# Linear attention and a SiLU MLP on one core: the second matmul moved into its own chunk, and heads regrouped

## The chip, the cores and the metric

The kernel runs on one core of one Trainium2 chip. The metric is the device time of one execution in microseconds; the time before is the median of three runs. One further execution was recorded by the hardware profiler, and the profile's times are counted from the start of its span.

A core has five engines with instruction streams of their own, each strictly in order: TensorE (PE in the profile, its weight loads PEld), VectorE (DVE), ScalarE (ACT), GpSimd (POOL) and SyncE (SP, which here only issues DMAs). Sixteen DMA engines move data between DRAM and the on-chip memory SBUF for all issuing engines. Matmuls write to PSUM, which has eight banks of 512 float32 columns.

## The reference

```python
def _attn_ref(q, k, v):            # each (8, 8, 576, 64): batch, head, position, 64
    q_s = softmax of q over the last axis
    k_s = softmax of k over the positions (axis 2)
    kv = np.einsum('bhsd,bhse->bhde', k_s, v)
    return np.einsum('bhsd,bhde->bhse', q_s, kv)

def reference(q, k, v, moe_w_in, moe_w_out):
    x = attention, heads side by side          # 4608 tokens x 512
    h = x @ moe_w_in                           # 512 x 2048
    g = h * (1 / (1 + exp(-h)))
    return g @ moe_w_out                       # 2048 x 512, float32
```

The softmaxes are written out in the original with a maximum subtracted and 1e-9 added to the sum.

## The kernel before

**Attention, batch by batch.** `load` brings q, k and v of a batch as tiles of 128 partitions: eight heads are four groups (`NG`) of two, a group's first head lies in partitions 0 to 63 and its second in 64 to 127, and each partition holds nine positions of 64 numbers (2304 bytes in DRAM). `exp` (ACT) makes `eq` and `ek` in bfloat16, `qsum` (DVE) the sums of `eq` and their reciprocals, `qnorm` multiplies them in (DVE or POOL), `vcast` casts v and leaves a column of ones beside it. `tr_dma` (L119) transposes `eq` to `qT` by one DMA from SP; batch 0 is transposed on TensorE instead (`tr`, `trcopy`). `kv` (L144) multiplies `ek` with v: 18 matmuls over 64 partitions for each half `cc` of the groups, into `kvps`, which has two PSUM banks of its own. `kvcopy` (L157) divides by the key sums (the column of ones) and puts the two heads of a chunk on the diagonal of a 128x128 block of `kvbd`, one block for each of the four chunks `c` of the 512 features. `xt` (L172) multiplies `qT` with these blocks and so gives `XT`, the tokens' attention output with features in partitions; it writes PSUM tile `o1` (one bank), and ACT copies it.

**MLP, chunk by chunk of tokens.** There are nine chunks: chunk 0 is batch 0 (576 tokens, in parts of 320 and 256), chunk 1 has 448 tokens, the others 512. `mm1(t, fb)` (L196) is one unit of the first matmul: four matmuls into a bank `hps`, tanh on ACT, and a multiply on DVE that writes `GT` (L216). There are 16 units `fb` for a chunk. The second matmul also has 16 units of four matmuls for a chunk: `mm2(t, tb, part, nparts)` (L228) takes the four 128-token tiles `tb` one after the other, each in four quarters of the contraction, so that two banks `ops` suffice; chunk 0 alone uses `mm2_wide` (L323), which does all four tiles for one `fc` at a time. `store` (L243) evicts a finished tile and writes it out by two DMAs of 64 partitions each.

**The order is written out by hand** (`manual_schedule`). A list `units` holds mm1 and mm2 units: mm1(0), mm2(0) and mm1(1) stand one after the other, mm2(1) follows and its second half alternates with mm1(2); from chunk 3 on mm1(t) alternates with mm2(t-1), and mm2(8) comes last, alone. `plan_attn` (L376) hangs the steps of a batch's attention on units before the start of the chunk that needs them; each engine's stream, SP's and POOL's too, follows this order. PSUM is divided into three banks `hps` (also used by `tr` and chunk 0's `xt`), two `ops`, one `aps` (for `o1`) and two `kvps`.

**The weights** come by DMAs from POOL, which cast to bfloat16: `W1` in 16 DMAs of 64 partitions (L279), since a chunk's 128 rows belong to heads that aren't neighbours in `w_in`, then `W2` in four DMAs (L284). A one-element copy on POOL (L273) makes them wait for the first half of batch 0's v; another (L399) makes batch 1's loads wait for the last piece of W1. Batch 2's q is loaded next on SP, ahead of batch 1's transpose. `heat` (L291) issues matmuls on a zero tile at the start.

## Time and profile before

| | |
|---|---|
| median of three runs | 305.15 us (304.4 to 307.14) |
| the profiled execution | 307.5 us |
| its span, first to last instruction | 305.7 us |
| TensorE busy | 281.9 us, 92% of the span |
| DVE / ACT / POOL busy | 148.9 / 162.5 / 52.3 us |
| DMA | 46.34 MB, mean 152 GB/s |
| granted TensorE clock, mean | 0.983 |

The profile's page cuts the span into 40 slices and gives each engine's busy share in tenths (9 means 90% or more); the DMA row is the mean share of the 16 DMA engines. The answer by stretches gives, for each stretch of time, its length and then the busy time of PE, PEld, DVE, ACT and POOL with the number of instructions in brackets, the granted clock (1.00 is full speed), the DMA share (contended packets can bring it above 1) and the GB/s. The chain of work that ended last is followed back from the last instruction, each step to what released it: start, length and what it was. A row of the timeline has start, length, engine, line, operation, output and inputs, how many instructions were merged, and in brackets the idle time before the first of them and what ended it. A row of the DMA queues has packets, MB and the packets' time as a share of 16 engines; q1 is the queue of SP, q0 that of POOL. The busy time of TensorE counts the modelled ends of pipelined matmuls.

### The profile page before, as it was taken

The page shows a single profiled execution, that of the slowest core. Times are in us where ns is not written, and L with a number is a line of the kernel's source. Part 1 is how long each engine was busy: PE and PEld are TensorE (multiplying, and loading weights), DVE is VectorE, ACT ScalarE, POOL GpSimd, SP SyncE. Part 2 cuts the span into 40 slices and gives each one's busy share as a digit, 9 for nine tenths or more (in the row PEclk, how much of TensorE's full clock was granted, in tenths as well). Part 3 has the DMA queues.
Part 4 walks back from the last instruction along what each step waited for, and adds up shares of the span by engine and source line. Part 5 has one row for each costly group of instructions (what it writes and reads, how often), then busy time and mean ns, then how long its engine had stood idle before and what let it go on. Part 6 is the DMA issues. An engine that isn't in the chain of part 4 may idle for free.

```text
span 305.7 us, 4237 instructions
## 1 busy us (share of the span) xinstructions
PE 281.9 (92%) x1597; PEld 135.2 (44%) x1597; DVE 148.9 (49%) x280; ACT 162.5 (53%) x266; POOL 52.3 (17%) x52
## 2 busy tenths in 40 slices
PE   5679995878999799989999999999999999999993
PEld 1546642434444344444444444444444444444441
DVE  4858884277355666543564366343533343343200
ACT  4647741577585686644765566543363445443320
POOL 0753000025080251700080017000000000000000
PEclk9579999999999999999999999999999999999999
DMA  7999999998959905961496142115111111112122
GB/s 268 259 141 159 282 312 289 348 392 246 346 198 243 362 2 104 341 202 35 82 326 240 34 93 55 35 36 112 36 34 34 34 36 34 34 40 56 44 69 69
DMA packets 39268, 46.34 MB, mean 152 GB/s; under 512 B 18256, under 2 KB 22352, under 8 KB 39248
## 3 DMA queue, kind: packets, MB, share of 16 engines
q1 hardware_dynamic: 34832, 41.88, 45.7%
q0 software_dynamic: 4416, 4.20, 9.3%
q8 instruction: 12, 0.20, 0.3%
q14 instruction: 8, 0.07, 0.1%
HBM read 36.70 MB, written 9.44 MB: 151 GB/s over the span
## 4 chain that ended last, share of the span: by engine, by line
PE 74%; DMA 15%; DVE 4%; ACT 2%; POOL 2%; issue 1%; SPq 1%; ACTq 0%; DVEq 0%; POOLq 0%
PE ops L233 35%; PE hps L200 34%; DMA vt<-in_v_dram 8%; DMA W_58<-in_moe_w_in_dram 4%; DMA qT<-eq 3%; PE kvps L149 2%; POOL W_58 L279 1%; DVE GT L216 1%; DVE zq L103 1%; PE ops L329 1%; ACT sg L208 1%; ACT eq L89 1%; SPq L80 0%; DVE kvbd_62 L163 0%; ACT XT L192 0%
## 5 line engine op out<-in xcount | busy, mean ns | idle before, releaser
L216 DVE SCALAR_TENSOR_TENSOR GT<-sg,hps 128x512 bf16<-128x512 f32 (+2 forms) x176 | 100.4, 586 | 114.4 <-ACT sg L208 113.5
L200 PE MATMUL hps<-XT,W_58 128*128 128x512 bf16 (+3 forms) x640 | 147.0, 361 | 3.7 <-DVE GT L216 2.7
L208 ACT ACTIVATE sg<-hps 128x512 f32<-128x512 f32 (+3 forms) x160 | 88.3, 554 | 96.4 <-PE hps L200 94.9
L233 PE MATMUL ops<-W_59,GT 128*128 128x512 bf16 x512 | 128.6, 379 | 0.0
L200 PEld LDWEIGHTS <-W_58 128*128 128x128 bf16 x640 | 61.7, 99 | 70.0 <-issue 7.4
L233 PEld LDWEIGHTS <-GT 128*128 128x128 bf16 x512 | 48.9, 98 | 55.7
L109 POOL TENSOR_TENSOR eq<-eq,rzq 128x1152 bf16<-128x1152 bf16 x12 | 25.4, 2117 | 123.0 <-ACT eq L89 56.8
L248 ACT ACTIVATE ost<-ops 128x512 f32<-128x512 f32 x34 | 20.2, 598 | 19.4 <-PE ops L233 19.4
L103 DVE TENSOR_REDUCE zq<-eq 128x18 f32<-128x1152 bf16 x16 | 21.6, 1348 | 7.9 <-ACT eq L89 7.9
L89 ACT ACTIVATE ek<-kt 128x1152 bf16<-128x1152 f32 x16 | 18.4, 1156 | 5.7 <-DMA kt<-in_k_dram 5.7
L89 ACT ACTIVATE eq<-qt 128x1152 bf16<-128x1152 f32 x16 | 18.4, 1159 | 2.4 <-DMA qt<-in_q_dram 2.4
L149 PEld LDWEIGHTS <-ek 64*128 64x128 bf16 x288 | 9.2, 99 | 13.0 <-issue 6.9
L329 PE MATMUL ops<-W_59,GT 128*128 128x512 bf16 x64 | 14.9, 379 | 0.0
L279 POOL DMA_DIRECT2D W_58<-in_moe_w_in_dram x16 | 9.7, 642 | 3.2 <-DMA W_58<-in_moe_w_in_dram 3.1
L329 PEld LDWEIGHTS <-GT 128*128 128x128 bf16 x64 | 6.2, 98 | 8.9 <-issue 2.0
L149 PE MATMUL kvps<-vaug_61,ek 64*128 64x130 bf16 x144 | 5.5, 217 | 3.9 <-DVE vaug_61 L96 2.3
L149 PE MATMUL kvps<-vaug_60,ek 64*128 64x130 bf16 x144 | 6.4, 240 | 2.7 <-ACT vaug_60 L94 1.3
L96 POOL CAST vaug_61<-vt 128x1152 bf16<-128x1152 f32 x6 | 6.8, 1157 | 0.0
L96 POOL CAST vaug_60<-vt 128x1152 bf16<-128x1152 f32 x6 | 6.8, 1155 | 0.0
L293 PE MATMUL wps<-warm 128*128 128x512 bf16 x11 | 4.8, 599 | 1.2 <-DVE warm L258 1.2
L109 DVE TENSOR_TENSOR eq<-eq,rzq 128x1152 bf16<-128x1152 bf16 x4 | 5.4, 1357 | 0.1
L132 PE MATMUL qtps<-ident,eq 128*128 128x128 bf16 x18 | 2.3, 313 | 3.3 <-DVE eq L109 3.3
(137 smaller groups left out, 80.2 us busy)
## 6 DMA issues: line engine op xcount, KB each, us to landing
out_dram<-ost SPq DMA_DIRECT2D x72, 128.0 KB, 2.4
qt<-in_q_dram SPq DMA_DIRECT2D x7, 1152.0 KB, 6.5
kt<-in_k_dram SPq DMA_DIRECT2D x7, 1152.0 KB, 8.4
vt<-in_v_dram SPq DMA_DIRECT2D x7, 1152.0 KB, 11.7
W_58<-in_moe_w_in_dram POOLq DMA_DIRECT2D x16, 128.0 KB, 6.5
W_59<-in_moe_w_out_dram POOLq DMA_DIRECT2D x4, 512.0 KB, 14.5
qt<-in_q_dram SPq DMA_DIRECT2D x2, 576.0 KB, 4.1
kt<-in_k_dram SPq DMA_DIRECT2D x2, 576.0 KB, 7.4
```

The source lines that it names most:

```text
L89: nc.scalar.activation(out=o, in_=jgd(st[b][src], cc), func=ACT.Exp)
L96: eng.tensor_copy(o, jgd(st[b]["vt"], cc))
L103: nc.vector.reduce_sum(out=st[b]["zq"][:, cc], in_=e, axis=AX.X)
L109: eng.tensor_tensor(out=e, in0=e, in1=r[:, :, :, None].to_broadcast([128, J, 2, D]), op=ALU.mult)
L149: nc.tensor.matmul(out=st[b]["kvps"][:, r, cc * 256:cc * 256 + 2 * E1], lhsT=st[b]["ek"][r * P:(r + 1) * P, j, cc * 128:(cc + 1) * 128], r ...
L200: nc.tensor.matmul(out=hps[:, 0:size], lhsT=W1[:, c, fb * 128:(fb + 1) * 128], rhs=XT[t][:, c, off:off + size], start=(c == 0), stop=(c == ...
L208: nc.scalar.activation(out=sg[:, 0:size], in_=hps[:, 0:size], func=ACT.Tanh, scale=0.5)
L216: nc.vector.scalar_tensor_tensor(out=GT[g][:, fb, col:col + n], in0=sg[:, h], scalar=1.0, in1=hps[:, h], op0=ALU.add, op1=ALU.mult,)
L233: nc.tensor.matmul(out=OP[t, tb], lhsT=GT[t][:, fc, tb * 128:(tb + 1) * 128], rhs=W2[:, fc, :], start=(fc == 0), stop=(fc == NFB - 1),)
L248: nc.scalar.activation(out=ost, in_=OP[t, tb], func=ACT.Copy, scale=0.5)
L279: nc.gpsimd.dma_start(out=W1[g * 64:(g + 1) * 64, 2 * cc:2 * cc + 2, i * FQ:(i + 1) * FQ], in_=w_in_v[g][:, cc, :, i * FQ:(i + 1) * FQ],)
L329: nc.tensor.matmul(out=OP[t, tb], lhsT=GT[t][:, fc, tb * 128:(tb + 1) * 128], rhs=W2[:, fc, :], start=(fc == 0), stop=(fc == NFB - 1),)
```

## The change

- A unit of mm2 of chunk t now runs inside chunk t: mm1(t) leads by six units (`LAG`), then mm2 and mm1 units alternate. Chunk 0 does this by itself; chunks 1 to 8 run through in one alternating sequence.
- `mm2(t, i)` takes quarter `i // 4` of the contraction for tile `i % 4`, so that all four tiles are open at once in four banks `ops`, and all four finish in the last four units. Odd tiles are evicted by DVE, even ones by ACT. `mm2_wide` is gone.
- PSUM: four banks `ops` and one ring of four banks for everything else: `hps`, `o1`, `tr`'s tiles, and kv's result, which is now two tiles of one bank.
- `kvcopy` handles the two tiles separately: two reciprocals and four multiplies in place of one and two.
- Heads: chunk c now holds heads 2c and 2c+1, so a chunk's rows of `w_in` are 128 neighbouring rows. In return a load of q, k or v is cut into four DMAs of 64 partitions (two halves `cc`, two heads `r`). Batch 0's q and its first half of k are shared between the queues of SP and ACT.
- Weights: W1 in four DMAs of 128 partitions, in the order W1(0), W1(1), W2(0), W1(2), W2(1), W1(3), W2(2), W2(3). Batch 1's loads wait for W2(1).
- More `heat` matmuls (24, 5, 1 and 2 in place of 10 and 1), and other offsets for the attention steps; batch 1's `qnorm` goes to POOL, its `vcast` stays on DVE.

```diff
@@ -63,21 +63,17 @@
 
     ctx.enter_context(tc.manual_schedule())
 
-    def view(t, b, cc=None):
...
     st = [dict() for _ in range(B)]
 
-    def load(b, name, src, cc=None):
+    def load(b, name, src, ccs=(0, 1), engs=(nc.sync, nc.sync)):
         if name not in st[b]:
             st[b][name] = ld.tile([128, NG, J * D], FP32, name=name)
-        t = st[b][name]
-        if cc is None:
-            nc.sync.dma_start(out=t, in_=view(src, b))
-        else:
-            nc.sync.dma_start(out=t[:, 2 * cc:2 * cc + 2, :], in_=view(src, b, cc))
+        x = src[b].rearrange("(c r g) (p j) d -> c r p g (j d)", r=2, g=2, j=J)
+        for cc in ccs:
+            for r in range(2):
+                engs[r].dma_start(
+                    out=st[b][name][r * P:(r + 1) * P, 2 * cc:2 * cc + 2, :], in_=x[cc, r]
+                )
 
     def jgd(t, cc):
         return t[:, 2 * cc:2 * cc + 2, :].rearrange("p g (j d) -> p j g d", d=D)
@@ -125,7 +121,7 @@
     TG = 6
 
     def tr(b, g):
-        t = ps.tile([128, TG, 128], BF16, name="qtps", tag="hps", bufs=PSB["hps"])
+        t = ps.tile([128, TG, 128], BF16, name="qtps", tag="ring", bufs=PSB["ring"])
         st[b]["qtps", g] = t
         for i in range(TG):
             cc, j = divmod(g * TG + i, J)
@@ -142,12 +138,12 @@
             i += n
 
     def kv(b, cc):
-        if "kvps" not in st[b]:
-            st[b]["kvps"] = ps.tile([128, 2, 512], FP32, name="kvps", tag="kvps", bufs=1)
+        t = [ps.tile([128, 512], FP32, name="kvps", tag="ring", bufs=PSB["ring"]) for _ in range(2)]
+        st[b]["kvps", cc] = t
         for j in range(J):
             for r in range(2):
                 nc.tensor.matmul(
-                    out=st[b]["kvps"][:, r, cc * 256:cc * 256 + 2 * E1],
+                    out=t[r][:, 0:2 * E1],
                     lhsT=st[b]["ek"][r * P:(r + 1) * P, j, cc * 128:(cc + 1) * 128],
                     rhs=vaug[b % 2][r * P:(r + 1) * P, j, cc * 2 * E1:(cc + 1) * 2 * E1],
                     start=(j == 0),
@@ -155,26 +151,26 @@
                 )
 
     def kvcopy(b, cc):
-        kp = st[b]["kvps"][:, :, cc * 256:cc * 256 + 2 * E1]
-        rz = ap.tile([128, 2, 2], FP32, name="rz")
-        nc.vector.reciprocal(out=rz, in_=kp[:, :, D::E1])
-        for g in range(2):
-            h = slice(g * 64, (g + 1) * 64)
-            nc.vector.tensor_tensor(
-                out=kvbd[b % 3][h, 2 * cc:2 * cc + 2, g * 64:(g + 1) * 64],
-                in0=kp[h, :, g * E1:g * E1 + D],
-                in1=rz[h, :, g:g + 1].to_broadcast([64, 2, D]),
-                op=ALU.mult,
-            )
+        for r in range(2):
+            kp = st[b]["kvps", cc][r]
+            rz = ap.tile([128, 2], FP32, name="rz", bufs=4)
+            nc.vector.reciprocal(out=rz, in_=kp[:, D:2 * E1:E1])
+            for g in range(2):
+                h = slice(g * 64, (g + 1) * 64)
+                nc.vector.tensor_scalar_mul(
+                    out=kvbd[b % 3][h, 2 * cc + r, g * 64:(g + 1) * 64],
+                    in0=kp[h, g * E1:g * E1 + D],
+                    scalar1=rz[h, g:g + 1],
+                )
 
     XT = {}
 
-    def xt(t, c, tag="aps", dve=0):
+    def xt(t, c, tags=("ring", "ring"), dve=0):
         if t not in XT:
             XT[t] = mp.tile([128, NC, S], BF16, name="XT")
         cc, r = divmod(c, 2)
         for i, (off, size) in enumerate(part[t]):
-            o1 = ps.tile([128, TCH], FP32, name="o1", tag=tag, bufs=PSB[tag])
+            o1 = ps.tile([128, TCH], FP32, name="o1", tag=tags[i], bufs=PSB[tags[i]])
             a = first = cut[t] + off
             while a < first + size:
                 b, col = divmod(a, S)
@@ -195,7 +191,7 @@
 
     def mm1(t, fb):
         for off, size in part[t]:
-            hps = ps.tile([128, TCH], FP32, name="hps", tag="hps", bufs=PSB["hps"])
+            hps = ps.tile([128, TCH], FP32, name="hps", tag="ring", bufs=PSB["ring"])
             for c in range(NC):
                 nc.tensor.matmul(
                     out=hps[:, 0:size],
@@ -225,11 +221,13 @@
 
     OP = {}
 
-    def mm2(t, tb, part, nparts):
-        if part == 0:
+    def mm2(t, i):
+
+        qd, tb = divmod(i, 4)
+        if qd == 0:
             OP[t, tb] = ps.tile([128, DM], FP32, name="ops", tag="ops", bufs=PSB["ops"])
-        n = NFB // nparts
-        for fc in range(part * n, (part + 1) * n):
+        n = NFB // 4
+        for fc in range(qd * n, (qd + 1) * n):
             nc.tensor.matmul(
                 out=OP[t, tb],
                 lhsT=GT[t][:, fc, tb * 128:(tb + 1) * 128],
@@ -237,8 +235,8 @@
                 start=(fc == 0),
                 stop=(fc == NFB - 1),
             )
-        if part == nparts - 1:
-            store(t, tb)
+        if qd == 3:
+            store(t, tb, tb % 2)
 
     def store(t, tb, dve=0):
         ost = mp.tile([128, DM], FP32, name="ost", bufs=4)
@@ -251,18 +249,20 @@
             rows = out[b * S:(b + 1) * S, :].rearrange("(p j) o -> j p o", j=J)[col // P]
             nc.sync.dma_start(out=rows, in_=ost[i * P:(i + 1) * P, :])
 
-    PSB = {"hps": 3, "ops": 2, "aps": 1}
+    PSB = {"ring": 4, "ops": 4}
 
 
     nc.vector.memset(dummy, 0.0)
     nc.vector.memset(warm, 0.0)
     nc.scalar.activation(out=dummy, in_=dummy, func=ACT.Exp)
     make_identity(nc, ident_f)
+    both = (nc.sync, nc.scalar)
     for cc in range(2):
-        load(0, "qt", q, cc)
-    for cc in range(2):
-        load(0, "kt", k, cc)
-        load(0, "vt", v, cc)
+        load(0, "qt", q, (cc,), both)
+    load(0, "kt", k, (0,), both)
+    load(0, "vt", v, (0,))
+    load(0, "kt", k, (1,))
+    load(0, "vt", v, (1,))
     nc.vector.tensor_copy(ident, ident_f)
     for t in vaug:
         nc.vector.memset(t.rearrange("p j (g e) -> p (j g) e", e=E1)[:, :, D:E1], 1.0)
@@ -270,29 +270,41 @@
         nc.vector.memset(t, 0.0)
 
 
-    nc.gpsimd.tensor_copy(gate[:, 0:1], st[0]["vt"][0:1, 1, 0:1])
     FQ = DFF // 4
-    w_in_v = w_in.rearrange("(c g r d) f -> g d c r f", g=2, r=2, d=D)
-    for i in range(4):
-        for g in range(2):
-            for cc in range(2):
-                nc.gpsimd.dma_start(
-                    out=W1[g * 64:(g + 1) * 64, 2 * cc:2 * cc + 2, i * FQ:(i + 1) * FQ],
-                    in_=w_in_v[g][:, cc, :, i * FQ:(i + 1) * FQ],
-                )
-    for i in range(4):
+
+    def load_w1(i):
+        nc.gpsimd.dma_start(
+            out=W1[:, :, i * FQ:(i + 1) * FQ],
+            in_=w_in[:, i * FQ:(i + 1) * FQ].rearrange("(c p) f -> p c f", p=128),
+        )
+
+    def load_w2(i):
         nc.gpsimd.dma_start(
             out=W2[:, i * 4:(i + 1) * 4, :],
             in_=w_out[i * FQ:(i + 1) * FQ, :].rearrange("(fc p) o -> p fc o", p=128),
         )
 
+    nc.gpsimd.tensor_copy(gate[:, 0:1], st[0]["vt"][0:1, 1, 0:1])
+    load_w1(0)
+    load_w1(1)
+    load_w2(0)
+    load_w1(2)
+    load_w2(1)
+    load_w1(3)
+    load_w2(2)
+    load_w2(3)
+    st[1]["qt"] = ld.tile([128, NG, J * D], FP32, name="qt")
+    nc.gpsimd.tensor_copy(st[1]["qt"][0:1, 0, 0:1], W2[0:1, 4, 0:1])
+    for name, src in (("qt", q), ("kt", k), ("vt", v)):
+        load(1, name, src)
+
     wps = ps.tile([128, 512], FP32, name="wps", tag="ops", bufs=PSB["ops"])
 
     def heat(n):
         for _ in range(n):
             nc.tensor.matmul(out=wps, lhsT=warm[:, 0:128], rhs=warm, start=True, stop=True)
 
-    heat(10)
+    heat(24)
     for cc in range(2):
         exp(0, "qt", "eq", cc)
         qsum(0, cc)
@@ -303,77 +315,41 @@
     vcast(0, 1, nc.scalar)
     tr(0, 0)
     trcopy(0, 0)
+    heat(5)
     kv(0, 0)
     kvcopy(0, 0)
     heat(1)
     for g in (1, 2):
         tr(0, g)
         trcopy(0, g)
+    heat(2)
     kv(0, 1)
     kvcopy(0, 1)
     for c in range(NC):
-        xt(0, c, "hps", 1)
-
-
+        xt(0, c, ("ring", "ops"), 1)
+
+
+
+    LAG = 6
     units = []
 
-    def add_mm1(t):
...
-    add_mm2(NCH - 1)
+    def add(first, last):
+        x = [(("mm1", t), lambda t=t, i=i: mm1(t, i)) for t in range(first, last) for i in range(NFB)]
+        y = [(("mm2", t), lambda t=t, i=i: mm2(t, i)) for t in range(first, last) for i in range(NFB)]
+        units.extend(x[:LAG])
+        for i in range(len(y)):
+            units.append(y[i])
+            units.extend(x[LAG + i:LAG + i + 1])
+
+    add(0, 1)
+    add(1, NCH)
     begin = {t: next(u for u, f in enumerate(units) if f[0] == ("mm1", t)) for t in range(NCH)}
     at = [[] for _ in units]
 
     def plan(u, f):
         at[u].append(f)
 
-    def plan_attn(b, u, sm, tp, ks, ox, eng=(nc.gpsimd, nc.gpsimd)):
+    def plan_attn(b, u, sm, tp, ks, ox, eng=(nc.gpsimd, nc.gpsimd), veng=nc.gpsimd):
 
 
 
@@ -382,7 +358,7 @@
             plan(u + sm[cc] + 1, lambda cc=cc: (qsum(b, cc), qnorm(b, cc, eng[cc])))
         for cc in range(2):
             plan(u + sm[2 + cc], lambda cc=cc: exp(b, "kt", "ek", cc))
-            plan(u + sm[2 + cc], lambda cc=cc: vcast(b, cc, eng[cc]))
+            plan(u + sm[2 + cc], lambda cc=cc: vcast(b, cc, veng))
         plan(u + tp, lambda: tr_dma(b, nc.sync))
         if b == 1:
             plan(u + tp, lambda: [load(2, n, x) for n, x in (("kt", k), ("vt", v))])
@@ -394,19 +370,12 @@
         for c in range(NC):
             plan(u + ox[c], lambda c=c: xt(b, c))
 
-
-    st[1]["qt"] = ld.tile([128, NG, J * D], FP32, name="qt")
-    nc.gpsimd.tensor_copy(st[1]["qt"][64:65, 0, 0:1], W1[64:65, 3, DFF - 1:DFF])
-    for name, src in (("qt", q), ("kt", k), ("vt", v)):
-        load(1, name, src)
-    plan(14, lambda: load(2, "qt", q))
     V = nc.vector
-    plan_attn(1, begin[1], (-14, -12, -10, -9), -6, (-5, -4), (-4, -3, -2, -1), (V, V))
-    plan_attn(2, begin[2], (-21, -17, -13, -9), -9, (-7, -5), (-4, -3, -2, -1))
-    plan_attn(3, begin[3], (-26, -24, -22, -20), -13, (-9, -7), (-6, -5, -4, -3))
-    plan_attn(4, begin[4], (-42, -38, -34, -30), -20, (-12, -10), (-9, -7, -5, -3))
-    for b in range(5, B):
-        plan_attn(b, begin[b], (-56, -52, -48, -44), -22, (-13, -11), (-9, -7, -5, -3))
+    plan(begin[1] - 8, lambda: load(2, "qt", q))
+    plan_attn(1, begin[1], (-16, -14, -10, -9), -7, (-4, -3), (-3, -2, -1, 0), (nc.gpsimd, nc.gpsimd), V)
+    plan_attn(2, begin[2], (-27, -24, -20, -16), -14, (-9, -7), (-5, -4, -3, -2))
+    for b in range(3, B):
+        plan_attn(b, begin[b], (-48, -44, -40, -36), -22, (-15, -11), (-9, -7, -5, -3))
     for c in range(NC):
         plan(begin[NCH - 1] - 9 + 2 * c, lambda c=c: xt(NCH - 1, c))
 
```

## The prediction

> **What bounds the kernel now.** I read the page's 40 slices first (a slice is 7.64 us), then the stretches by stage, then the chain of work that ended last, then the DMA queues.
>
> ```profile
> PE   5679995878999799989999999999999999999993
> DMA  7999999998959905961496142115111111112122
> ```
> ```profile
> 38.20:58.50 20.30, 16.14 (x106) 7.56 (x104) 10.05 (x18) 7.04 (x11) 0.00 (x0) 1.00 1.10 305
> 58.50:73.80 15.30, 12.62 (x65) 6.18 (x64) 12.14 (x20) 11.72 (x20) 5.37 (x4) 1.00 0.95 353
> 73.80:84.30 10.50, 10.23 (x82) 5.00 (x81) 4.17 (x11) 6.00 (x11) 1.05 (x1) 1.00 1.03 311
> 84.30:110.30 26.00, 23.58 (x142) 10.98 (x141) 15.82 (x28) 18.39 (x29) 11.41 (x7) 1.00 0.73 233
> 110.30:135.00 24.70, 23.43 (x141) 11.00 (x140) 13.29 (x24) 15.29 (x24) 7.89 (x6) 1.00 0.61 190
> 188.00:218.00 30.00, 30.00 (x175) 14.04 (x174) 12.34 (x22) 14.95 (x26) 1.61 (x2) 1.00 0.26 55
> ```
>
> In the second fence the first figure after the stretch is its length, the next is TensorE's busy time. From 135 us to the last matmul TensorE is always busy: a chunk takes 30.0 us, and 32 units of 0.864 us (four matmuls of 512 columns, from the chain), two kv blocks of 0.69 and four xt of 0.22 make 29.9. Reordering can gain nothing there. All that can be won lies before 135 us: between 58.5 and 135 TensorE is idle for 2.68 + 0.27 + 2.42 + 1.27 = 6.6 us, and before 58.5 the DMA row is full. The chain says what the early part waits for:
>
> ```profile
> 22.14 5.55 DMA W_58<-in_moe_w_in_dram
> 29.12 16.71 DMA vt<-in_v_dram
> 45.84 8.44 DMA qT<-eq
> ```
>
> Chunk 1 needs batch 1, whose loads wait until all of W1 has landed (27.8 us), share the DMA engines with W2, and end at about 50.5; then the DMA transpose of qT lands at 54.3, and four xt, each followed by four matmuls, lead to chunk 1's first mm1 at 58.5. Whatever TensorE does faster before that only waits longer.
>
> **Part 1: the early order and the loads.** Chunk 0's second matmul now runs inside its first one. TensorE's work up to batch 1's xt is the same: from about 19.5 us (the first steady mm1 now is at 19.1), six units alone at 1.0 us, ten pairs at 0.97 + 0.86, three units, one kv: it stands still at about 47 to 49 us. So the start of chunk 1 (call it T1) stays a DMA sum, which I take from these rows.
>
> ```profile
> q0 software_dynamic: 2468, 2.27, 102.9%
> ...
> q0 software_dynamic: 372, 0.37, 113.4%
> ...
> q1 hardware_dynamic: 1091, 2.44, 58.9%
> q0 software_dynamic: 1091, 1.08, 53.1%
> ...
> q1 hardware_dynamic: 362, 0.80, 101.9%
> ```
>
> They are packets per queue in 12 to 28 us (W1 in 16 pieces), 30 to 32 (W2 in whole pieces), 32 to 44 (both queues) and 46 to 48 (loads alone). Without the packets under 512 B, weights go at 138 a us in 64-partition pieces, at 183 in whole ones; in the mix each queue moves 88 a us; loads alone 172. The weights are 4096 packets of 2 KB read, a batch's q, k and v 3 x 512 of 2304 B. W1 becomes whole, but keeps its strided rows, so I take 160 a us between the ends. Batch 1 is now released by the fifth of eight pieces, 2560 packets: 12 + 2522/160 = 27.8, landed 1.2 later as W1 is now, first load packet another 3.5 later (now: issue 28.0, packets from 31.5): 32.5. By then 3312 weight packets are through. The other 784 take 784/88 = 8.9 us, with as many load packets; then 1536 + 512 (batch 2's q stands ahead of the transpose on SP, as now) - 784 = 1264 at 172 take 7.3: 48.7, against 50.5 now, -1.8 us. At 138 the same sum gives 51.8 (+1.3), at 183 it gives 46.2 (-4.3). I take **T1 -1.5**, the mean of the ends, with both kept.
>
> Whether halves load as fast as whole tiles is the open price. A load of one tensor is now four DMAs of 64 partitions, not one of 128. The nearest rows are the output stores, which are 64 partitions already:
>
> ```profile
> DMA packets 464, 0.78 MB, mean 392 GB/s; under 512 B 91, under 2 KB 91, under 8 KB 463
> ...
> q1 hardware_dynamic: 463, 0.77, 101.7%
> ```
> ```profile
> DMA packets 160, 0.26 MB, mean 175 GB/s; under 512 B 32, under 2 KB 32, under 8 KB 160
> ...
> q1 hardware_dynamic: 160, 0.26, 75.1%
> ```
>
> The first is 69.5 to 71.5 us, stores in a backlog: 16 engines x 2 us x 1.017, less 91 small packets of 9 ns, over 372 packets is 85 ns for 2 KB. The second is 216.5 to 218, one pair of stores alone: 141 ns. Loads stand in a backlog, so I take the first row: no price. The other end, a factor 1.66 on a load packet's 93 ns, is a rival below. The Trainium skill speaks against the change here: "DMA: Bandwidth & Descriptors", section "Rules for kernel authors", says two transfers to disjoint partition halves serialize and one 128-partition transfer should be used, and "SBUF — State Buffer", section "Door 1: The DMA port swizzle", puts 64 partitions at 196 GB/s against 328. By that page the 1264 packets alone would cost some 62 ns each (93 x 328/196 - 93), an estimate of 4.9 us; the isolated pair agrees with it, the backlog row doesn't.
>
> The small edits of the start (14 + 5 + 2 more warm-up matmuls at 0.43 us cold or 0.22 warm, three loads issued on ACT, which is idle until 4.4 us, four-piece copies of kv) move TensorE's start by -0.5 to +4 us. The wait for qT, which I expect at 48.7 + 3.8 = 52.5, hides 3.5 us of that; beyond, it costs one for one. POOL issues 8 weight DMAs at 0.76 us in place of 16 at 0.64 and 4 at 0.76 (6.1 us for 13.3), ahead of nothing that is late. SP issues 12 DMAs a batch at 0.47 to 0.52 us (6 us, 288 KB each 0.5 us, more than the engines move), with the transpose and the stores behind them; the stores have four buffers and a chunk of time.
>
> **Part 2: from T1 to 135 us.** The idle 6.6 us come from stretches of mm1 without mm2:
>
> ```profile
> 66.68 3.19 PE L200 MATMUL hps<-XT,W_58 128*128 128x448 bf16 x16 [1.12 <-DVE GT L216]
> 70.93 3.19 PE L200 MATMUL hps<-XT,W_58 128*128 128x448 bf16 x16 [1.06 <-DVE GT L216]
> ```
>
> Here mm1 takes 0.756 us a unit, DVE 0.62, and a reduction with its reciprocal (1.35 + 0.27) stands between, so three hps banks run out. With the change only six such units stand alone after T1; then each has an mm2 unit beside it, and there are four banks. What is late next: in those six units DVE has 6 x 0.62 + 2 x 1.62 = 7.0 us of work against 4.5 of TensorE; four banks and the first mm2 leave about 1.5 us of stall. The crowded heads of batches 2 and 3 (two exp of 1.16 in one unit, xt in four consecutive units) leave another 1.1. So 2.6 of 6.6 stay: **-4.0**; bounds -1.5 (the crowd stays late) to -5.6 (1 us left).
>
> **Part 3: steady state.** Units, matmuls and pairing are as now. The ring of four holds hps, xt's o1 and two kv banks. kvcopy grows from 0.18 + 2 x 0.29 to 2 x 0.18 + 4 x about 0.21 (the 128x64 multiply at 37.86 us took 0.21): 1.2 us. Its wait stands on DVE ahead of the next GT multiply. Worst order: GT 0.69, reduction 1.62, kvcopy 1.2 = 3.5 us, against four units of 0.864 = 3.5 until the next kv wants the banks. So about 0, with 0.2 a kv at most; the 12 kv after T1 are inside Part 2's bounds.
>
> **Part 4: the end.** Now the four tiles of the last chunk finish 3.46 us apart; then 0.864 apart, with eight DMA issues of 0.515 us on SP, 4.1 us against 3.5, and the last eviction on DVE (0.69 for 0.60): **+0.7**, from 0 to +1.2.
>
> **Sum.** -1.5 - 4.0 + 0.7 = -4.8. The profiled execution took 307.5 us with a span of 305.7: 302.7. The median of the runs is 305.15, 2.35 below that execution; on its scale **300.4**. Bounds of this case: -9.9 to +1.0, 295 to 306.
>
> **Rivals.**
> - *Halves load at the slow rate.* For: the isolated pair of stores. Against: the backlog row. 1264 packets x 61 ns / 16 = +4.8 on T1, and batch 2's k, v and batch 3's loads come 2560 x 61 / 16 = 9.8 us late at exps that stand at most 8 us behind T1: some 2.5 us of ACT and then TensorE. 300.4 + 7.3 = 307.7. It cancels the gain from about 133 ns a packet.
> - *The ring stalls* (the slower side). kv takes two of four banks and returns them through DVE; if one reduction or one exp more comes ahead of kvcopy, the next kv or hps waits 1.2 to 1.6 us. At half of 12 kv, 6 x 1.4 = 8.4: 308.8. It decides from 0.4 us a kv, where 12 x 0.4 eat the 4.8. For: the same wait exists now at 100.7 us (1.53 us on kvbd). Against: Part 3's count.
> - *It doesn't do what it says.* The first chunks' idle time is that of batches 1 to 3 arriving late, and it moves instead of going: T1 0, -1.0, +0.7: 304.9. For: DMA is full until 75 us. Against: the waits above name DVE, not a load.
>
> **How the numbers follow.** Forecast 0.47, slow halves 0.20, moved idle 0.21, ring 0.12. About 1% (3.05 us) is what a measurement of this kernel can tell from no change. Faster: 0.43 of the forecast's case and 0.03 of the moved one, 0.46. Slower: 0.10 of the slow halves (with weights at 138 they give 310), 0.09 of the ring, 0.02 elsewhere, 0.21. The rest is 0.33. The range leaves out one in ten a side: 296 to 308.8.
>
> **What would show it.** First mm1 of chunk 1 near 57 us; load packets alone near 93 ns; hps waiting on GT under 3 us between T1 and 135 us; a chunk at 30.0 us; the last matmul some 5.5 us before the end. Wrong if load packets take over 130 ns, if kvps or o1 waits on DVE or ACT in every chunk, or if warm-up or batch 0 brings TensorE to batch 1's xt after qT has landed.

## The result, and the profile after

The changed kernel takes 314.75 us (median of 4 runs, 312.93 to 317.49); the kernel before took 305.52 us beside it (4 runs, 304.40 to 307.14). The ratio is 1.0305, with a 95% interval of 1.0215 to 1.0396. The forecast was 300.4 us, its range 296 to 308.8, so the measured time lies outside it. The rival *slow halves* named the right cause, with 307.7 us, and was still 7 us short. Of the ten executions of one kernel below (*before, four whole DMAs*) two ran in a slower state; its ratio leaves them out, its median doesn't.

In what follows a load in *halves* is one by DMAs of 64 partitions, as in the change, and a *whole* load one by DMAs of 128. T1 is the start of chunk 1's first mm1.

The profiled execution of the changed kernel was its fastest, 312.93 us, with a span of 311.2 us; that of the kernel before was 307.5 us with 305.7. These two traces differ by 5.5 us of span, less than the medians, and the first part of what follows explains 5.5 us. The experiments add the rest.

The page's slices come first (one is 7.78 us; DMA busy share in tenths):

```profile
PE   8559985889689999999999999999999999999992
...
DMA  7999999999999898289838974500450050014005
```

TensorE's row now has its weak slices at 2 and 3 (5 and 5; before, the weak ones were 1 and 2), the old hole at slice 7, and a new one at slice 11. The DMA row, which had its first gaps at slices 10 to 13 (8, 9, 5, 9), is now full to slice 13 and not under 8 until slice 17: the same 46 MB take longer. The chain of work that ended last says for whom (start, length, what):

```profile
30.63 6.29 DMA qt<-in_q_dram
...
36.94 11.34 DMA vt<-in_v_dram
...
48.34 9.47 DMA qT<-eq
...
61.91 8.74 DMA qt<-in_q_dram
...
70.67 8.58 DMA vt<-in_v_dram
...
79.27 1.93 DMA out_dram<-ost
...
81.67 4.77 DMA qT<-eq
```

Before, the chain ended its DMA part with batch 1's qT at 54.3 us. Now it goes through batch 1's qT at 57.8, and then through loads once more, to batch 2's qT at 86.4. TensorE's rows show both, and the row of before for T1 stands first (start, busy time, line, operation, in brackets the wait ahead of it and what ended it):

```profile
58.53 5.61 PE L200 MATMUL hps<-XT,W_58 128*128 128x448 bf16 x28
```
```profile
53.06 1.55 PE L145 MATMUL kvps<-vaug_61,ek 64*128 64x130 bf16 x18 [3.01 <-DVE GT L212]
...
57.94 0.35 PE L178 MATMUL o_724<-qT,kvbd_63 128*128 128x448 bf16 x1 [0.88 <-DMA qT<-eq]
...
61.88 4.16 PE L196 MATMUL hps<-XT,W_58 128*128 128x448 bf16 x20
...
86.48 0.32 PE L178 MATMUL o_1020<-qT,kvbd_64 128*128 128x384 bf16 x1 [3.81 <-DMA qT<-eq]
```

T1, the first mm1 of chunk 1, is at 61.88 us (58.53 before): +3.35. From T1 to the last matmul's end it is 243.5 us against 242.3: +1.2. From there to the end 5.8 against 4.85: +1.0. Together 5.5.

**Loads run at three fifths of their speed.** The DMA view of 40 to 50 us, where batch 1's loads are nearly alone:

```profile
DMA packets 1227, 2.51 MB, mean 251 GB/s; under 512 B 140, under 2 KB 150, under 8 KB 1225
...
q1 hardware_dynamic: 1214, 2.48, 103.2%
```

1214 less 140 small packets are 1074 load packets in 10 us: 107 a us, where 46 to 48 us of the kernel before had 172 a us and 406 GB/s. Their time, 16 engines x 10 us x 1.032 less 140 small ones at 9 ns, is 153 ns a packet; it was 93. The prediction's own sign for this ("wrong if load packets take over 130 ns") is in the trace. 251 over 406 GB/s is 0.62. The Trainium skill's "SBUF — State Buffer", section "Door 1: The DMA port swizzle", has 196 GB/s for 64 partitions against 328 for 128, which is 0.60, and its "DMA: Bandwidth & Descriptors", section "Rules for kernel authors", says to use one 128-partition transfer. The ratio measured here agrees with the page's; both rates are higher here.

**SP holds batch 2's transpose.** The timeline of SP's DMA issues (start, time from the first to the end of the last, line, how many):

```profile
55.97 2.55 SPq L74 DMA_DIRECT2D kt<-in_k_dram  x4
58.62 2.55 SPq L74 DMA_DIRECT2D vt<-in_v_dram  x4
61.27 3.11 SPq L74 DMA_DIRECT2D qt<-in_q_dram  x4
65.01 3.97 SPq L74 DMA_DIRECT2D kt<-in_k_dram  x4
69.58 3.80 SPq L74 DMA_DIRECT2D vt<-in_v_dram  x4
73.92 7.64 SPq L250 DMA_DIRECT2D out_dram<-ost  x8
81.67 2.78 SPq L116 DMA_TRANSPOSE qT<-eq  x1
```

POOL had finished the second half of batch 2's q, the transpose's input, at 71.7 us:

```profile
69.57 2.12 POOL L105 TENSOR_TENSOR eq<-eq,rzq 128x1152 bf16<-128x1152 bf16 x1 [0.95 <-DVE rzq L100]
```

The transpose issues 10 us later, behind twenty loads (batch 2's k and v, batch 3's q, k and v) and eight stores. SP issues the last store at 81.1 us and the transpose directly behind it. The loads ahead hold it up themselves: four issues take 2.55 us at first and 3.97 later, and of SP's waits from 60 to 82 us 8.5 us are put down to earlier loads that had yet to land. TensorE then waits 3.81 us, and pays again, for after the wait the granted clock is lower. Stretches of the changed kernel (length, TensorE busy; after POOL's count stand the granted clock, the DMA share and GB/s):

```profile
84.00:86.00 2.00, 0.00 (x0) 0.00 (x0) 0.00 (x0) 0.00 (x0) 0.00 (x0) 1.00 1.02 190
86.00:88.00 2.00, 1.52 (x7) 0.70 (x7) 0.00 (x0) 0.59 (x1) 0.00 (x0) 0.79 0.97 257
88.00:90.00 2.00, 2.00 (x9) 0.95 (x7) 0.00 (x0) 1.49 (x2) 0.00 (x0) 0.50 1.04 244
90.00:92.00 2.00, 2.00 (x11) 0.91 (x10) 0.62 (x1) 1.41 (x4) 0.00 (x0) 0.86 1.06 252
92.00:94.00 2.00, 2.00 (x12) 0.94 (x10) 0.62 (x1) 0.79 (x2) 0.00 (x0) 1.00 1.06 256
```

**The steady state** has a chunk of 30.43 us, not 30.0. This period is counted from the first kv of one batch to that of the next:

```profile
107.85:138.29 30.44, 30.28 (x175) 14.14 (x174) 17.83 (x34) 16.69 (x27) 6.43 (x4) 1.00 0.75 172
138.29:168.73 30.44, 30.27 (x175) 14.17 (x174) 17.84 (x34) 16.68 (x27) 6.43 (x4) 1.00 0.77 171
```

and its timeline says why:

```profile
138.29 0.68 PE L145 MATMUL kvps<-vaug_60,ek 64*128 64x130 bf16 x18
...
139.62 1.35 DVE L99 TENSOR_REDUCE zq<-eq 128x18 f32<-128x1152 bf16 x1
...
141.40 0.58 DVE L160 TENSOR_SCALAR kvbd_63<-kvps,rz 64x64 bf16<-64x64 f32 x2
...
142.22 0.58 DVE L160 TENSOR_SCALAR kvbd_63<-kvps,rz 64x64 bf16<-64x64 f32 x2
...
142.86 0.68 PE L145 MATMUL kvps<-vaug_60,ek 64*128 64x130 bf16 x17 [0.17 <-DVE kvbd_63 L160]
```

kv's copies stand on DVE behind a reduction of the next batch, and the second kv waits for the bank that they free.

### The profile page after: what moved, and what is told of

Read it like the earlier page. It is cut to its first block, busy times and chain, and to the rows that moved or that the text cites. A ratio compares the mean times of both kernels' runs of the same rounds, so it can differ in the third digit from the quotient of the medians.

```text
span 311.2 us, 4432 instructions
## 1 busy us (share of the span) xinstructions
PE 286.4 (92%) x1618; PEld 137.6 (44%) x1618; DVE 166.2 (53%) x342; ACT 152.4 (49%) x250; POOL 50.0 (16%) x42
## 4 chain that ended last, share of the span: by engine, by line
PE 65%; DMA 24%; DVE 5%; POOL 1%; ACT 1%; SPq 1%; issue 1%; DVEq 0%
PE ops L231 32%; PE hps L196 30%; DMA vt<-in_v_dram 9%; DMA W_59<-in_moe_w_out_dram 5%; DMA qt<-in_q_dram 5%; DMA qT<-eq 5%; DVE zq L99 2%; PE kvps L145 1%; DVE GT L212 1%; ACT sg L204 1%; POOL W_58 L276 1%; DVE kvbd_62 L160 1%; SPq L74 1%; DMA out_dram<-ost 1%; DVE kvbd_63 L160 1%
## 5 line engine op out<-in xcount | busy, mean ns | idle before, releaser
L231 PE MATMUL ops<-W_59,GT 128*128 128x512 bf16 x576 | 148.4, 382 | 0.0
L105 POOL TENSOR_TENSOR eq<-eq,rzq 128x1152 bf16<-128x1152 bf16 x14 | 29.6, 2117 | 137.6 <-ACT sg L204 95.6
L244 DVE TENSOR_SCALAR ost<-ops 128x512 f32<-128x512 f32 x18 | 12.3, 686 | 6.7 <-PE ops L231 6.7
L246 ACT ACTIVATE ost<-ops 128x512 f32<-128x512 f32 x18 | 10.8, 597 | 10.2 <-PE ops L231 10.2
L145 PE MATMUL kvps<-vaug_60,ek 64*128 64x130 bf16 x144 | 6.5, 225 | 5.4 <-ACT vaug_60 L90 4.9
L305 PE MATMUL wps<-warm 128*128 128x512 bf16 x32 | 9.5, 453 | 1.2 <-DVE warm L256 1.2
L145 PE MATMUL kvps<-vaug_61,ek 64*128 64x130 bf16 x144 | 6.7, 228 | 3.5 <-DVE GT L212 3.0
L157 DVE RECIPROCAL rz<-kvps 128x2 f32<-128x2 f32 x32 | 4.9, 154 | 4.2 <-PE kvps L145 3.7
L160 DVE TENSOR_SCALAR kvbd_63<-kvps,rz 64x64 bf16<-64x64 f32 x24 | 6.8, 283 | 0.6
L160 DVE TENSOR_SCALAR kvbd_62<-kvps,rz 64x64 bf16<-64x64 f32 x24 | 6.8, 283 | 0.6
L305 PEld LDWEIGHTS <-warm 128*128 128x128 bf16 x32 | 3.5, 114 | 5.7 <-issue 2.6
```

What stands on the lines that cost most here:

```text
L105: eng.tensor_tensor(out=e, in0=e, in1=r[:, :, :, None].to_broadcast([128, J, 2, D]), op=ALU.mult)
L145: nc.tensor.matmul(out=t[r][:, 0:2 * E1], lhsT=st[b]["ek"][r * P:(r + 1) * P, j, cc * 128:(cc + 1) * 128], rhs=vaug[b % 2][r * P:(r + 1) * ...
L160: nc.vector.tensor_scalar_mul(out=kvbd[b % 3][h, 2 * cc + r, g * 64:(g + 1) * 64], in0=kp[h, g * E1:g * E1 + D], scalar1=rz[h, g:g + 1],)
L231: nc.tensor.matmul(out=OP[t, tb], lhsT=GT[t][:, fc, tb * 128:(tb + 1) * 128], rhs=W2[:, fc, :], start=(fc == 0), stop=(fc == NFB - 1),)
L244: nc.vector.tensor_scalar_mul(out=ost, in0=OP[t, tb], scalar1=0.5)
L305: nc.tensor.matmul(out=wps, lhsT=warm[:, 0:128], rhs=warm, start=True, stop=True)
```

## The experiments

**The halves, and what is left without them.** First, the changed kernel with one DMA of 128 partitions a tensor. In this and all later kernels with whole loads, batch 0's loads that were split between SP and ACT go to SP alone (code is shortened here and below, with `...` or a comment where something is left out):

```diff
-        x = src[b].rearrange("(c r g) (p j) d -> c r p g (j d)", r=2, g=2, j=J)
-        for cc in ccs:
-            for r in range(2):
-                engs[r].dma_start(out=st[b][name][r * P:(r + 1) * P, 2 * cc:2 * cc + 2, :], in_=x[cc, r])
+        x = src[b].rearrange("(g r) (p j) d -> g (r p) (j d)", r=2, j=J).rearrange("g x y -> x g y")
+        nc.sync.dma_start(out=st[b][name], in_=x)        # batch 0: one for each cc
```

> The changed kernel with q, k and v loaded as before, one DMA over 128 partitions for a tensor (batch 0 by halves cc), all from SP; everything else is the change's. The heads then lie in other rows than W1's, so the output is that of another pairing of heads and rows; times are not touched by that. Theory 1 (loads of 64 partitions are slow, 150 ns a packet for 93): load packets back at 93 ns where they are alone, chunk 1's first mm1 near 56 us in place of 61.9, no 3.8 us wait for the second qT near 82 us, the chunk period stays at 30.4; 302 to 305 us in place of 314.75. Theory 2 (the ring and the order of the heads' steps cost the time): the period and the waits stay, 312 or more.

Measured: 302.61 us, 0.987 of before (0.9797 to 0.9944). T1 is at 57.13, load packets alone take 96 ns (38 to 46 us), and there is no wait for batch 2's qT, whose transpose issues at 68.45:

```profile
68.45 3.21 SPq L117 DMA_TRANSPOSE qT<-eq  x1
```

The second kernel also takes W1 in its 16 old pieces, so that the heads are paired as before:

```diff
-        nc.gpsimd.dma_start(out=W1[:, :, i * FQ:(i + 1) * FQ], in_=...)
+        for g in range(2):
+            for cc in range(2):
+                nc.gpsimd.dma_start(out=W1[g * 64:(g + 1) * 64, 2 * cc:2 * cc + 2, i * FQ:(i + 1) * FQ], in_=w_in_v[g][:, cc, ...])
```

> The changed kernel with the heads as before: whole loads, and W1 in 16 DMAs of 64 partitions, in the new order of pieces. So the order of mm1 and mm2, the ring, the offsets and the warm-up stay changed. Theory 1: nearly all of the loss comes from the regrouped loads, and whole W1 pieces are worth 1 to 3 us: 304 to 308 us. Theory 2: 312 or more.

Measured: 302.75 us, 0.9901 (0.9865 to 0.9937); T1 at 57.07. So with one DMA a tensor whole pieces of W1 are worth nothing that shows, the halves cost 12.1 us (314.75 - 302.61), and all the rest of the change gains about 3 us.

The other way round, the kernel before with the loads in halves and W1 in four pieces, and nothing else:

```diff
+        x = src[b].rearrange("(c r g) (p j) d -> c r p g (j d)", r=2, g=2, j=J)
+        for c in (0, 1) if cc is None else (cc,):
+            for r in range(2):
+                nc.sync.dma_start(out=st[b][name][r * P:(r + 1) * P, 2 * c:2 * c + 2, :], in_=x[c, r])
...                                                   # W1 by four DMAs, as in the change
```

> The kernel before with the regrouped heads alone: every load in DMAs of 64 partitions, all from SP, W1 in four whole DMAs ahead of W2; order, PSUM and offsets as before. Theory 1: 6 to 10 us over the kernel before (312 to 316). Theory 2: within 2 us of it, the whole W1 pieces paying for the loads.

Measured: 318.48 us, 1.0414 (1.0355 to 1.0472). Load packets alone take 166 ns (48 to 54 us), T1 is at 66.67. The price in the old order of the work is 12.7 us, nearly the same in sum, so the rest of the change isn't needed for it. In the traces it is paid elsewhere: 8.1 us by T1 and 2.5 behind it.

**Is it the half, or the number of DMAs?** Four DMAs a tensor, as in the change, but each of 128 partitions:

```diff
...                                  # x as in the first kernel, for every cc:
+            for g in range(2 * cc, 2 * cc + 2):
+                nc.sync.dma_start(out=st[b][name][:, g:g + 1, :], in_=x[:, g:g + 1, :])
```

> The changed kernel with its four DMAs a tensor kept, but each of 128 partitions and one group of heads (2304 B a partition) instead of 64 partitions and two groups; all issues on SP; W1 in whole pieces, so that the heads meet other rows of W1 (the output is that of another pairing of the heads, the work is the same). Same bytes, same packets, same number of issues. Theory (the partition half is what costs): load packets alone 93 to 105 ns, T1 near 57, 302 to 304 us. Rival (it is the number of issues, or 288 KB being too little in flight for one DMA): packets at 140 ns or more, or gaps between the DMAs of about 0.2 us x 12 a batch; T1 at 61 or later, 310 us or more.

Measured: 299.84 us, 0.9804 (0.9741 to 0.9867). Its DMA view from 40 to 45 us:

```profile
DMA packets 974, 1.99 MB, mean 399 GB/s; under 512 B 109, under 2 KB 109, under 8 KB 974
...
q1 hardware_dynamic: 974, 1.99, 104.7%
```

865 load packets in 5 us are 173 a us, at 16 x 5 x 1.047 us less 109 x 9 ns, or 96 ns each. The same bytes, packets and number of issues on the same queue, and full speed: the partition half is the cause. T1 came at 53.73 here, earlier than with large loads, and I took that for a second gain. The same split in the kernel before tests it:

```diff
-            nc.sync.dma_start(out=t, in_=view(src, b))
...
+        for g in range(NG) if cc is None else range(2 * cc, 2 * cc + 2):
+            nc.sync.dma_start(out=t[:, g:g + 1, :], in_=view(src, b)[:, g:g + 1, :])
```

> The kernel before with nothing but four DMAs a tensor (batch 0: two a part) of 128 partitions and one group of heads each, in place of one. Theory (splitting a load into whole-partition DMAs helps any order of the work, since its DMA queue gets a larger share beside the weights): T1 falls from 58.5 to about 55.5, 302 to 303 us. Rival (it helps only where TensorE can use the earlier batch 1; in the kernel before TensorE reaches batch 1's xt at about 54 anyway, or the share is no larger): 305 to 306, no change.

Measured: 307.78 us, 1.0044 (1.0004 to 1.0083), T1 at 58.38 against 58.53. Splitting gains no time there; the theory fell. The trace has a reason that the rival didn't name: TensorE's wait for batch 1's qT ends at 52.48 us, 1.8 us earlier than before, but behind this wait of 2.65 us the granted clock is 0.50 from 53 to 56 us, and the way from there to T1 takes 5.9 us in place of 4.2.

**Where the price is paid.** Whole loads for the first batches, halves for the others (`if b < 2` or `if b < 3` ahead of the two ways to load):

> The changed kernel with whole loads for batches 0 and 1 only; batches 2 to 7 still come in 64-partition DMAs; W1 in whole pieces (the heads of batches 0 and 1 meet other rows of W1: another pairing's output, the same work). It splits the price of the halves by place. Theory (most of the price is paid at T1 and before, a smaller part where batches 2 and 3 arrive late): T1 near 57.5, then a wait for batch 2's qT of 2 to 5 us with the lower clock behind it; 306 to 309 us. Rival 1 (all of it is paid by T1): 302 to 303, no wait after T1. Rival 2 (nearly all of it is paid by batches 2 and 3): 311 to 315.

Measured: 309.94 us, 1.0107 (1.0068 to 1.0146). T1 is at 57.17, and the wait after it is the largest of all:

```profile
83.62 0.48 PE L187 MATMUL o<-qT,kvbd 128*128 128x384 bf16 x1 [5.66 <-DMA qT<-eq]
```

So 7.3 of the 12.1 us (309.94 - 302.61) can be paid behind T1 alone, and 4.8 (314.75 - 309.94) by T1. In the changed kernel, with T1 at 61.88, the wait is 3.81. A later T1 alone doesn't explain the smaller wait: with T1 at 64.08 one of 5.43 us appears below.

> The changed kernel with whole loads for batches 0 to 2; only batches 3 to 7 come in 64-partition DMAs; W1 in whole pieces (the heads of batches 0 to 2 meet other rows of W1: another pairing's output, the same work). Theory (the price is paid only while the loads are behind the work; from chunk 3 on a batch's 3.5 MB take 14 us of 30): 302 to 303.5, as with whole loads throughout. Rival 1 (batch 3's halves, issued ahead of batch 2's transpose, are what makes it late): 305 to 308 with a wait for batch 2's qT. Rival 2 (halves also cost in the steady state, by slower stores or banks that come free later): a period above 30.43 us and 304 or more without such a wait.

Measured: 304.00 us, 0.9955 (0.9927 to 0.9983), T1 at 55.72, period as with whole loads, and a wait of 1.90 us for batch 2's qT, although batch 2's own loads are whole. What is in halves then is batch 3's load, issued ahead of batch 2's transpose (at 73.63 us, against 68.45 with whole loads). Rival 1 holds in kind, at a smaller price; from chunk 3 on halves cost nothing that shows: from T1 to the end it takes 1.9 us more than with whole loads (245.9 against 244.0), which is that wait.

The queue by itself: the changed kernel, with batch 3's k and v issued behind batch 2's transpose:

```diff
-        if b + 2 < B:
+        if b == 1:
+            plan(u + tp + 1, lambda: load(3, "qt", q))
+        if b == 2:
+            plan(u + tp + 1, lambda: [load(3, n, x) for n, x in (("kt", k), ("vt", v))])
+        if 1 < b < B - 2:
             plan(u + tp + 1, lambda: [load(b + 2, *x) for x in (("qt", q), ("kt", k), ("vt", v))])
```

> The changed kernel, halves and all, with eight of batch 3's twelve load DMAs (k and v) issued behind batch 2's transpose instead of ahead of it. Theory (batch 2's qT is late because its transpose stands on SP behind twenty load DMAs and the stores, and SP holds them back while so many are in flight at the slow rate): the transpose issues at about 75 us in place of 81.7, the wait for batch 2's qT of 3.8 us falls under 1 us, and the time falls by 3 to 6 us, to 309 to 312. Rival (the DMA engines are what is short, and whatever is issued first delays the other): the wait moves to batch 3's k or v, and the time stays at 314 to 315.

Measured: 312.32 us, 1.0212 (1.0162 to 1.0262), 2.4 us under the changed kernel; the two intervals overlap, so the traces must carry the reading. The SP queue:

```profile
57.88 2.56 SPq L74 DMA_DIRECT2D kt<-in_k_dram  x4
60.54 2.54 SPq L74 DMA_DIRECT2D vt<-in_v_dram  x4
63.19 2.71 SPq L74 DMA_DIRECT2D qt<-in_q_dram  x4
66.56 9.41 SPq L250 DMA_DIRECT2D out_dram<-ost  x8
76.08 3.09 SPq L116 DMA_TRANSPOSE qT<-eq  x1
```

Although T1 was at 64.19 in this execution, 2.3 us later than in the trace of the changed kernel, the transpose issues 5.6 us earlier and no wait for batch 2's qT is left. The rival's wait appears too, at a smaller price. ACT waits for batch 3's k, which now comes behind the transpose; the next tanh and GT multiply are late by that, and TensorE waits for them ahead of batch 2's xt:

```profile
84.30 1.16 ACT L85 ACTIVATE ek<-kt 128x1152 bf16<-128x1152 f32 x1 [3.91 <-DMA kt<-in_k_dram]
...
86.60 0.38 PE L178 MATMUL o<-qT,kvbd 128*128 128x128 bf16 x2 [1.67 <-DVE GT L212]
```

Behind this shorter wait the granted clock stays at 1.00. From T1 to the end of the span it takes 245.4 us against 249.3. The 3.9 us are the old wait of 3.81 us and about 1.7 us of lower clock behind it, less the new 1.67.

**The steady state.** The changed kernel with the q and k steps of batches 3 to 7 two units earlier, first with halves, then with whole loads and the old W1 pieces:

```diff
-        plan_attn(b, begin[b], (-48, -44, -40, -36), -22, (-15, -11), (-9, -7, -5, -3))
+        plan_attn(b, begin[b], (-50, -46, -42, -38), -22, (-15, -11), (-9, -7, -5, -3))
```

> The changed kernel with the exp and reduction steps of batches 3 to 7 two units earlier, so that no reduction of the next batch stands on DVE right ahead of kvcopy. Theory 2 (kv waits for banks that kvcopy returns late, behind a reduction): the period falls from 30.4 to 30.0, 2 to 3 us less: 312. Theory 1 alone: the period is not bound by that, within 1 us of 314.75.

Measured: 314.67 us, 1.0289 (1.0228 to 1.035): no gain over the changed kernel. The period did fall, from 30.43 to 29.95 us; but in the profiled execution T1 was at 64.08 and the wait for batch 2's qT 5.43 us. The late loads, which vary more than this edit is worth, cover it in this trace.

> The changed kernel with one DMA of 128 partitions a tensor (batch 0: two), W1 in its 16 old pieces, and the q and k steps of batches 3 to 7 two units earlier. Theory (the extra 0.43 us a chunk comes from a reduction of the next batch that stands on DVE ahead of kv's copies; it is real time wherever the loads arrive early): the distance from kv to kv falls from 30.43 to about 30.0 us as in the run of the halves, T1 stays at 57.1, and six chunks of 0.43 make 2.6 us: about 300.1, 0.98 of before. Rival (the time of a chunk is set elsewhere, and the wait only moves): 302.7 again, with the period back at 30.4 or with a new wait of 0.4 us a chunk.

Measured: 300.96 us, 0.9836 (0.9781 to 0.9891). Its stretches from kv to kv have no idle time left:

```profile
128.28:158.23 29.95, 29.95 (x175) 14.19 (x174) 17.74 (x35) 16.76 (x26) 6.43 (x4) 1.00 0.60 175
158.23:188.17 29.94, 29.94 (x173) 14.12 (x173) 17.73 (x35) 16.76 (x26) 6.43 (x4) 1.00 0.59 173
```

From T1 to the end it takes 241.5 us, 2.4 less than with the old offsets (243.9). The median fell by 1.8 us and not 2.6. In the profiled execution T1 was 1.4 us later, and its span is 1.0 us shorter (300.0 for 301.0).

**T1: TensorE or DMA?** With whole loads TensorE stalls 5.3 us at 38 to 43 us behind GT multiplies that are queued on DVE behind a reduction that waits for batch 1's q, and is busy from there to T1. If that stall set T1, its removal would show:

```diff
-    plan_attn(1, begin[1], (-16, -14, -10, -9), -7, ...)
+    plan_attn(1, begin[1], (-12, -11, -8, -7), -6, ...)
```

> The kernel with whole loads, old W1 pieces and early reductions, and batch 1's exp and reduction of q 4 and 3 units later (-12, -11 for -16, -14), its k and v steps 3 and 2 later (-8, -7 for -10 and -9... the v copies with them), the transpose one unit later. Theory (TensorE's stall of 5.5 us ahead of T1 is of its own making: the GT multiplies are queued on DVE behind a reduction that waits for a load, and from there TensorE is busy without a gap until T1): the stall shrinks below 2 us, T1 comes 1 to 3 us earlier (54 to 56), and the time falls by as much: 298 to 299. Rival (T1 is a sum of DMA times, as the prediction had it; whatever TensorE does sooner it waits longer for qT): T1 stays at 57 within 0.5 us, with a wait for qT in place of the wait for GT, and the time is that of the kernel without this edit within 0.5 us.

Measured: 299.81 us, 0.9801 (0.9739 to 0.9863), which the intervals don't tell from the kernel without the edit. T1 is at 58.18 against 58.45, and in place of one wait there are these:

```profile
PE kvps L146 <- DVE vaug L93: 2.0, 1, 2.0
...
PE o L179 <- DMA qT<-eq: 1.1, 1, 1.1
PE hps L197 <- DVE GT L213: 1.1, 2, 0.8
PE hps L197 <- DMA W<-in_moe_w_in_dram: 0.9, 1, 0.9
```

T1 stayed, as the rival had it, but this doesn't settle the question, for the two executions differ in more than the edit. Batch 1's q was issued at 30.70 us here and at 28.68 there, and the granted clock was 0.50 from 50 to 56 us, where the other had 1.00 (its own 0.50 had been from 42 to 48). From that issue to T1 it takes 27.5 us against 29.8. So the edit may have gained 2 us that a later start of the loads took back. What the traces do show is that each of these waits for DMAs, in one place or another: the stall of 5.3 us stands behind a load of q, and without it TensorE waits for v, qT and W1.

**A version that beats both.** Whole loads in four DMAs a tensor, old W1 pieces, early reductions:

> The changed kernel with four DMAs a tensor of 128 partitions and one group of heads each, W1 in its 16 old pieces, and the q and k steps of batches 3 to 7 two units earlier. Theory (two gains that add: smaller whole loads brought T1 to 53.7 against 57.1 us for large ones, and the earlier reductions take 0.43 us off each of six chunks): T1 near 54, kv to kv 30.0, 297 to 298 us. Rival (the early T1 came from W1's whole pieces or from that one execution): T1 at 57 or later, 300 to 301 us.

Measured: 299.64 us, 0.9796 (0.9766 to 0.9826): 2% faster than before. T1 is at 57.31, as the rival had it, and the period 29.95; the time lies between the two forecasts, and the two gains didn't add. That doesn't show that four DMAs bring nothing. Batch 1's loads were issued at 31.83 us here and at 27.39 in the kernel with T1 at 53.73; from that issue to T1 both take about 26 us (25.5 and 26.3), the kernels with one DMA a tensor 27.5 to 29.9. Whether W1's old pieces or this execution made the issue late wasn't separated.

T1 and the two columns beside it come from the one profiled execution of each kernel, the medians from all of them:

| kernel | batch 1's q issued | T1 | T1 to end of span | median us | ratio to before |
|---|---|---|---|---|---|
| before | 28.0 | 58.5 | 247.2 | 305.52 | 1 |
| changed | 30.6 | 61.9 | 249.3 | 314.75 | 1.0305 |
| changed, early reductions | 30.9 | 64.1 | 248.5 | 314.67 | 1.0289 |
| changed, batch 3 behind | 31.1 | 64.2 | 245.4 | 312.32 | 1.0212 |
| halves from batch 2 | 28.7 | 57.2 | 251.2 | 309.94 | 1.0107 |
| halves from batch 3 | 27.2 | 55.7 | 245.9 | 304.00 | 0.9955 |
| whole loads | 27.3 | 57.1 | 244.0 | 302.61 | 0.9870 |
| whole loads, old W1 pieces | 28.8 | 57.1 | 243.9 | 302.75 | 0.9901 |
| whole loads, old W1 pieces, early reductions | 28.7 | 58.5 | 241.5 | 300.96 | 0.9836 |
| the last one, batch 1 later | 30.7 | 58.2 | 241.5 | 299.81 | 0.9801 |
| four whole DMAs, old W1 pieces, early reductions | 31.8 | 57.3 | 241.2 | 299.64 | 0.9796 |
| four whole DMAs | 27.4 | 53.7 | 243.6 | 299.84 | 0.9804 |
| before, halves | 29.8 | 66.7 | 249.7 | 318.48 | 1.0414 |
| before, four whole DMAs | 26.8 | 58.4 | 246.8 | 307.78 | 1.0044 |

## Why the prediction was wrong, step by step

**The failed step** is in Part 1: "Loads stand in a backlog, so I take the first row: no price." The backlog row was of stores, which read SBUF; the loads write it. With the isolated row's factor, 1.66, a load packet would have taken 154 ns; 153 were measured. (The isolated row's 141 ns still has its 32 small packets in it. Without them, as in the other row, it is 139 ns, a factor of 1.63 and 152 ns.) What this step left out cost 12.1 us.

**The rival's sum was short as well.** By T1 it had +4.8 us; the runs gave 4.8 (the median with whole loads for the first two batches against the changed kernel's), and the three traces of the changed kernel and its halved variants put T1 5 to 7 us behind 57.1. Behind T1 it had "some 2.5 us of ACT and then TensorE", counted from late exps. The exps were on time: batch 2's q was ready at 71.7 us. What was late was its transpose, in SP's queue. Part 1 named that queue ("with the transpose and the stores behind them") and cleared the stores, not the transpose. Measured: 5.4 us behind T1 in the changed kernel (249.3 - 243.9), 7.2 where T1 isn't late. It is a wait of 3.81 us and about 1.7 us of lower clock behind it; the latter is in no term of the prediction.

**T1 without halves** came out at 57.07 and 57.13 us, where -1.5 had given 57.0; that is luck in part. The DMA sum was near: qT was expected at 52.5 us and landed at about 52.0 (with old W1 pieces: issued at 47.33, 4.7 to landing). But TensorE came to batch 1's first xt at 53.12, after it and without a wait, which the prediction had named as a sign of being wrong. It was late there by a stall of 5.5 us for GT, behind a reduction that waits for batch 1's q. That the weights would take 160 packets a us was wrong, they came at 201 where they were alone in whole pieces (25 to 30 us of the changed kernel); yet with one DMA a tensor W1 whole or in 16 pieces gives the same T1. Eight executions with whole loads for the first two batches have T1 between 53.7 and 58.5. The bounds of the start, -0.5 to +4 us ahead of a wait for qT, held in the changed kernel: with its first mm1 at 21.9 us, against 19.1, TensorE still stood waiting at 57.9.

**Part 2** (-4.0, bounds -1.5 to -5.6) was right in sign and nearly in size. With whole loads, old W1 pieces and the old offsets TensorE is idle for 1.73 us from T1 to 127 us, where the kernel before had 6.64 to 135: -4.9. The six units alone behind T1 and four banks were the reason given, and in the changed kernel hps waits on GT for 0.82 us there.

**Part 3** (0) was mis-sized. A multiply of kvcopy took 0.283 us, where I took 0.21 from another one, so that a kvcopy is 1.5 us and not 1.2; the worst order that was counted, 3.5 us against 3.5, became the usual one and failed: the period is 30.43 us, and 29.95 with the reductions moved away, 0.48 us a chunk. The sign that the prediction gave, kvps waiting for DVE in every chunk, is in the trace (0.17 us). That is the rival *ring stalls* in kind and place, at a third of its price and once a chunk.

**Part 4** (+0.7, at most +1.2): 1.0 to 1.3 us, from the last matmul's end to the end of the span (changed kernel and whole loads against before). The last eight issues of the changed kernel take 4.97 us and not 4.1:

```profile
303.43 4.97 SPq L250 DMA_DIRECT2D out_dram<-ost  x8
...
305.40 0.69 DVE L244 TENSOR_SCALAR ost<-ops 128x512 f32<-128x512 f32 x1 [1.03 <-PE ops L231]
```

**The sum** without the halves was -4.8 on the profiled execution. Between the trace of before and that of the kernel with whole loads and old W1 pieces it is -4.7 (301.0 us of span for 305.7): -1.5 for T1, -4.9 for Part 2, +1.8 of idle time behind it, +1.2 at the end, and TensorE busy for 1.3 us less from T1 on, whose cause stays open. (This trace has 1269 of the 1295 matmul records that before has from T1 on, so some of its idle time may be missing records; the trace with early reductions has them all and is busy for 1.1 us less.) On the medians it is -3.0 (302.75 for the 305.8 measured beside it), since the execution of before that was profiled is 1.7 us above that median; to carry its whole gain over to the median was a step of its own, and wrong by those 1.7 us. With the halves, 12.1 us more. *It doesn't do what it says* is refuted by the same runs: the idle time went, and did not move.

## What to carry to other kernels

A layout that makes one tensor whole can cut another in halves: count the bytes of both, and take a transfer's rate only from a row with the same direction and the same partitions. Here 128 partitions for one weight matrix, loaded once, were bought with 64 partitions for all of q, k and v: eight batches of 3 x 1152 KB. Where an in-order queue issues loads well ahead of their use, look for the one small DMA behind them that is needed soon, and price the queue at the rate of the loads, not of the issues.

## What was not expected of the hardware

- Stores from 64 partitions don't show the loads' price: in the changed kernel from 79.5 to 81.5 us, 308 packets, nearly all of 2 KB, take 90 ns each at 319 GB/s in a backlog of stores, beside 153 ns for 2304 B of a load into 64 partitions. Why the two directions differ was not tried.
- A second queue doesn't help halves: from 4 to 10 us, with SP and ACT each loading other partitions, 687 packets take 146 ns each and both queues together move 264 GB/s; four whole DMAs on one queue move 360 GB/s from 4 to 9 us.
- The granted clock fell to 0.50 at no fixed point of a wait. In the changed kernel it fell at about 87.1 us, half a microsecond after the end of the 3.81 us; in the waits of 5.43 and 5.66 us (early reductions, halves from batch 2) it fell 2 to 2.5 us after their start. It was at 1.00 again 3.5 to 4 us after the end of each. Behind waits of 1.67 and 1.90 us (batch 3 behind, halves from batch 3) it stayed at 1.00.
